# A planner that fixes a fused attention and gated-MLP kernel's order gets new lengths, delays and DMA queue rules

## The chip, the cores and the metric

The kernel runs on one core of one Trainium2 chip. Its time is the device time of one execution in microseconds (us), as a median over several runs. TensorE (PE) multiplies matrices, VectorE (DVE), ScalarE (ACT) and GpSimd (POOL) do element-wise work, SyncE (SP) issues every DMA transfer of this kernel. The five engines run beside each other, each in the order in which its instructions were written, and wait for each other by semaphores.

## The reference

The inputs are q, k, v of 4 batches x 8 heads x 768 positions x 64, and three weight matrices, all float32. What must be computed, cut to what matters:

```python
scores = scale * np.matmul(q, k.transpose(0, 1, 3, 2))
keep = is_sink | in_window          # first n_sink=4 positions, or the last window=128
scores = np.where(keep, scores, -1000000000.0)
a = np.exp(scores - np.max(scores, axis=-1, keepdims=True))
a = a / (np.sum(a, axis=-1, keepdims=True) + 1e-09)
x = np.matmul(a, v).transpose(0, 2, 1, 3).reshape(B * S, H * D)   # 3072 x 512
gate = 1.0 / (1.0 + np.exp(-(x @ w_gate)))                        # 512 x 1536
return gate * (x @ w_val) @ w_out                                 # 1536 x 512
```

## The kernel before

The 3072 tokens are cut into 12 token groups of 256, and those into 8 chunks: four of one group, four of two (`CHUNKS`). For each group there are 8 attention units, one a head, so 96 units `u`. The first 20 units are "plain": float32 matmuls, of which one program row takes two passes in the profile. Later units split each operand into a high and a low half (`hi`, `kl`, `vhl`, `wt`) and run one pass a half. A unit is: load `qkT` and `v` (SP), scores (PE, into PSUM tile `a`), mask and row maximum (DVE, `P`), exp (ACT), reciprocal of the sum (DVE), scaling of `P` (POOL, ACT or DVE), turn (PE transposes `P`), copies and cuts (`wt`: ACT, DVE, POOL), PV (PE, `wt` with `vhl`, and `sk` with `vshl` for the sinks), and two additions (DVE) into `xf`.

The MLP runs over 12 slices `f` of the hidden width. Weights arrive as pairs of 32-bit words (`wst`, 3 buffers, 36 loads of 512 KB) and are decoded by `decode`: load, a multiplication on ACT, a shift (ACT, DVE or POOL), two bit operations on DVE. Chunk 0 (`feed_whole`) uses the decoded weights as they are, `m<-hi,ws` and `o<-ws,th`. `halve` then makes a high half that stays on chip and a low half that goes to DRAM (`wlo_d`); all other chunks load low halves again through 8 buffers `lo` (396 loads of 256 KB). The `lo` buffers lie in memory that the `wst` buffers held, so the first `lo` load (`fetch`, read of `DECODED`) waits for the last decode. `thirds` and the pair chunks are a Strassen-like variant that saves products.

No instruction is placed by hand. `Plan.run` plays the whole program through in a model of its own: each step has a priority, one or more ways (an engine, a length, a function), tiles that it reads and writes, and buffer slots. Whenever a modelled engine is free, the ready step of best priority goes to it, and the sequence in which this happens is the sequence in which the instructions are written. What a step costs is written where it is made (`vec`, `once`, `two`, `act`, `pool`, the numbers in `attend`). `LAT` is the delay from the end of one step to a step that depends on it, `NEXT` the same within one engine, `ISSUE`, `BULK` and the two lines with `dma_free` model the DMA queue. The planner writes filler matmuls (`m<-ident`, 128x128) on PE where PE would be free in its model during the first 130 us and the modelled activity is low. `hint` writes a branch hint on PE, DVE and SP for the branch behind the last instruction (`skip`: it jumps over `general`, which serves inputs of other sizes).

Every step goes through one helper, so nearly all instructions have one line in the profile (L620; L629 after the change), and tiles tell them apart.

Of the kernel before, what the change touches and what calls it, by code (L numbers as in the profile page):

```python
# [59 lines left out]
LAT = 180.0  # L60
BULK = 620.0
ISSUE = 550.0
# [3 lines left out]
NEXT = dict(PE=0.0, V=60.0, A=60.0, G=60.0, Q=0.0)  # L66
# [21 lines left out]
B_lo = 8  # L88
B_w2 = 2
# [223 lines left out]
class Plan:  # L313
# [39 lines left out]
    def run(self, warm, fill_ns, fill):  # L353
# [37 lines left out]
        while events:  # L391
            now = events[0][0]
            while events and events[0][0] <= now:
# [14 lines left out]
                for x in o.after:  # L408
                    x.before -= 1
                    same = len(x.ways) == 1 and x.ways[0][0] == on  # L410
                    x.ready = max(x.ready, now + (NEXT[on] if same else LAT))
                    if on != "PE":
                        x.sure = max(x.sure, now + LAT + (SURE_D if o.dma else SURE))
# [3 lines left out]
            for e in free:  # L417
                if free[e] > now:
                    continue
                held = []  # L420
                unsure = [] if e == "PE" else None
                while waiting[e] or unsure:
# [18 lines left out]
                    if unsure is not None and (  # L441
                        o.sure > now
                        or any(slots[k][v - 1][1] + LAT + SURE > now for k, v in need.items())
                    ):
                        unsure.append((key, o))
                        continue
# [77 lines left out]
                    for x in o.after:  # L524
                        x.todo -= 1
                        x.due = max(x.due, end + LAT)
# [23 lines left out]
def kernel(  # L550
# [84 lines left out]
    def act(cols, psum=False):  # L635
        return 120 + 0.9 * cols

    def pool(cols):
        return Port(170 + 2.17 * cols)
# [199 lines left out]
    WLO, LOADS, GROUPS, DECODED, READY, READY2 = (Fixed(None) for _ in range(6))  # L839

    def sinks(b, u):
        if not b:
# [7 lines left out]
            for t, x in enumerate(VS0):  # L850
                for y in range(2):
                    o = 64 * y + NS * t
                    dma(
                        u + 0.5, 91.0, lambda x=x, y=y, o=o: Q.dma_start(
# [23 lines left out]
    def load(u, b, h, t0, T, prev, L, vraw, vin, qkT, plain):  # L878
# [4 lines left out]
            u, 0.75 * n * R / D, lambda: Q.dma_start(out=qkT()[0:R, 0:n], in_=qk[b, h, 0:R, c0 : c0 + n]),  # L883
# [3 lines left out]
            u, 100.0 * L, lambda: Q.dma_start(  # L887
# [4 lines left out]
    def attend(u, b, h, t0, T, XR):  # L892
# [44 lines left out]
        for t in range(T):  # L937
# [28 lines left out]
            def exp(t=t):  # L966
# [5 lines left out]
            plan.op(u, [("PE", 10 + (4 * n / 2.4 + 6 if plain else 2 * mac(n)), scores)], qk_reads, [sc, (P, t)], busy=0.5 if plain else 0.9)  # L972
            plan.op(
                u, [("V", 260 if first else 535, top)],
                [sc, (MASKS, 3), (MASKS, min(t0 + t, 2))], [sc, (P, t), (NEGM, (u, t))],
            )
            plan.op(u, [("A", 410, exp)], [], [(P, t), (rs, t)])
# [19 lines left out]
        def mul():  # L997
            for t in range(T):
# [4 lines left out]
                ("A", 200, lambda: A.activation(  # L1003
                    out=rs()[:, 0:T], in_=rs()[:, 0:T], func=AF.Copy, scale=1.0, bias=1.0e-9
                )),
                ("G", Port(213), guard(G)), ("V", Port(100), guard(V)),
# [3 lines left out]
            u, [("V", 110, lambda: V.reciprocal(out=rs()[:, 0:T], in_=rs()[:, 0:T]))], [], [rs]  # L1010
        )
        plan.op(u, [("G", Port(660), share), ("A", 720, mul), ("V", Port(555), scale)], [rs], [P])

        if not plain:
# [11 lines left out]
                u, [("V", 180, lambda: V.transpose(  # L1026
# [10 lines left out]
                u, [("G", Port(610), spread(G)), ("V", two(W), spread(V))], [turned, OWN], [sk]  # L1037
# [35 lines left out]
        plan.op(u, [("PE", 30 + (T + plain) * 110, turn)], [P], [tp, wt], busy=0.45)  # L1073
# [11 lines left out]
        plan.op(u, [("G", Port(180 + 0.9 * Z * (T - f) * 128), split)], [], [wt])  # L1085
        plan.op(u, [("G", Port(180 + 0.9 * Z * T * 128), rest_of)], [], [wt])
# [105 lines left out]
        if y:  # L1192
# [8 lines left out]
            elif not pair_of[tn]:  # L1201
# [9 lines left out]
                copy(u, W, hi, xv, read, [(H1, i), (L1, i)], plain)  # L1211
# [44 lines left out]
    def decode(prio, src, whole):  # L1256
# [6 lines left out]
        plan.op(prio, [("Q", ISSUE, lambda: Q.dma_start(out=st(), in_=src))], [], [st], dma=1456.0)  # L1263
# [16 lines left out]
                ("G", Port(1340.0), lambda: G.tensor_scalar(  # L1280
# [38 lines left out]
    def spare(pr, f, k, x):  # L1319
        dma(  # L1320
            pr, 728.0, lambda: Q.dma_start(
# [497 lines left out]
```

## Time and profile before

| what | before |
|---|---|
| median of 3 runs | 771.19 us (770.46 to 771.49) |
| the profiled execution | 774.19 us |
| its span, first to last instruction | 772.5 us |
| PE busy | 749.1 us, 97% of the span |
| DVE, POOL, ACT busy | 607.5, 506.1, 472.0 us |
| mean granted TensorE clock | 0.998 of full speed |

The profile is of one execution, 3.0 us above the median. An engine's busy time includes the tail of each instruction that lies under the next one, so 97% for PE says where PE had something in flight, not that it streamed at its best. Idle time on another engine costs nothing by itself; what counts is whether PE waits.

### The profile page before, as it was taken

The numbers are of one execution on the slowest core, as the hardware profiler recorded it, in microseconds if no ns is written. First come the engines' busy times: TensorE is split into PE (matmuls) and PEld (weight loads), VectorE is DVE, ScalarE is ACT, GpSimd is POOL, SyncE is SP. The second block draws the span as 40 slices with busy tenths as digits, with TensorE's granted clock in tenths as the row PEclk, the third lists the DMA queues.
The fourth block names the chain that finished last, engine by engine and source line by source line (L and its number), as shares of the span: only waits on it lengthen the run. The fifth ranks groups of instructions, "written<-read, shape, count | busy, mean of one in ns | idle before, by whom it ended". The sixth has DMA issues, their size and how long they took to land.

```text
span 772.5 us, 16296 instructions
## 1 busy us (share of the span) xinstructions
PE 749.1 (97%) x4986; PEld 674.9 (87%) x4986; DVE 607.5 (79%) x1782; ACT 472.0 (61%) x1338; POOL 506.1 (66%) x647
## 2 busy tenths in 40 slices
PE   7999999999999999999999999999999999999995
PEld 6866777998989999989999988999999999999995
DVE  5979988996999999969988889778999884433333
ACT  7879888765765777737666665457776652322221
POOL 3654676887999999937777977557976855321210
PEclk9999999999999999999999999999999999999999
DMA  6898987999999877677767777867697655677662
GB/s 165 222 297 250 323 263 234 376 307 311 342 294 319 284 220 207 200 252 231 233 224 225 242 233 222 246 196 251 193 306 249 196 159 178 217 240 211 198 205 86
DMA packets 120879, 185.57 MB, mean 240 GB/s; under 512 B 23248, under 2 KB 45264, under 8 KB 120784
## 3 DMA queue, kind: packets, MB, share of 16 engines
q1 hardware_dynamic: 120784, 184.45, 75.9%
q8 instruction: 42, 0.69, 0.4%
q14 instruction: 53, 0.43, 0.2%
HBM read 159.24 MB, written 25.17 MB: 239 GB/s over the span
## 4 chain that ended last, share of the span: by engine, by line
PE 61%; DVE 11%; DMA 6%; POOL 3%; ACT 2%; issue 2%; SPq 0%; ACTq 0%; POOLq 0%; DVEq 0%
PE m L620 34%; PE a L620 16%; PE o L620 11%; DVE ws L620 2%; DMA wst<-in_moe_w_gate_dram 1%; DMA out_dram<-w 1%; DVE P L620 1%; DVE th L620 1%; DMA vraw<-in_vt_dram 1%; DMA lo<-wlo_d 1%; DVE vhl L620 1%; POOL wt L620 1%; DVE hi L620 1%; DVE gl L620 1%; DVE xf L620 1%
## 5 line engine op out<-in xcount | busy, mean ns | idle before, releaser
L620 PE MATMUL m<-ws,ws 128*128 128x256 f32 x1536 | 290.0, 284 | 0.6 <-DVE th L620 0.2
L620 PE MATMUL m<-ws,lo 128*128 128x256 f32 x1344 | 288.6, 283 | 1.9 <-DMA lo<-wlo_d 1.3
L620 PEld LDWEIGHTS m<-ws,ws 128*128 128x128 f32 x1536 | 244.9, 189 | 13.1 <-DVE th L620 1.0
L620 PEld LDWEIGHTS m<-ws,lo 128*128 128x128 f32 x1344 | 215.0, 189 | 3.1 <-DMA lo<-wlo_d 2.3
L620 POOL TENSOR_SCALAR_AFFINE_SELECT wt<-wt 128x512 fp32r<-128x512 f32 (+3 forms) x192 | 125.9, 657 | 43.5 <-DVE wt L620 18.7
L620 POOL TENSOR_TENSOR gl<-th,gh 128x512 fp32r<-128x512 f32 (+1 forms) x34 | 38.2, 1122 | 99.6 <-ACT gh L620 82.7
L620 ACT ACTIVATE P<-P,negm_all 128x144 f32<-128x144 f32 x192 | 78.9, 412 | 28.7 <-DVE negm_all L620 26.8
L620 ACT ACTIVATE th<-m 128x256 f32<-128x256 f32 x96 | 36.6, 382 | 75.5 <-DVE th L620 71.9
L620 DVE TENSOR_TENSOR cv<-m,cv 128x256 f32<-128x256 f32 x96 | 40.2, 418 | 52.4 <-ACT cv L620 34.8
L620 ACT CAST gh<-th 128x512 fp32r<-128x512 f32 (+1 forms) x82 | 42.9, 523 | 55.3 <-DVE th L620 53.7
L620 POOL TENSOR_TENSOR ws<-ws,ws 128x512 fp32r<-128x512 f32 (+1 forms) x53 | 66.6, 1262 | 9.8 <-DVE ws L620 6.9
L620 PE MATMUL o<-ws,gh 128*128 128x512 f32 x168 | 67.6, 403 | 0.0
L620 PE MATMUL o<-ws,gl 128*128 128x512 f32 x168 | 66.2, 394 | 0.0
L620 PE MATMUL o<-lo,gh 128*128 128x512 f32 x168 | 65.8, 391 | 0.0
L620 DVE CUSTOM_DVE_ANT_0 P<-a,am 128x144 f32<-128x144 f32 x192 | 58.3, 306 | 8.8 <-PE a L620 2.2
L620 PE MATMUL a<-wt,vhl 128*128 128x256 f32 (+2 forms) x282 | 61.0, 327 | 1.8 <-POOL wt L620 1.6
L620 POOL TENSOR_TENSOR kl<-qkT,hi 128x400 fp32r<-128x400 f32 (+1 forms) x56 | 59.2, 1057 | 1.8
L620 PEld LDWEIGHTS a<-wt,vhl 128*128 128x128 f32 x282 | 47.3, 189 | 10.5 <-POOL wt L620 4.1
L620 ACT CAST hi<-qkT 128x656 fp32r<-128x656 f32 (+1 forms) x70 | 49.2, 703 | 10.9 <-PE a L620 10.0
L620 POOL TENSOR_TENSOR P<-P,rs 128x288 f32<-128x288 f32 x46 | 35.1, 764 | 29.8 <-DVE rs L620 26.2
L620 POOL TENSOR_TENSOR hi<-qkT,hi 64x256 fp32r<-64x256 f32 x53 | 41.2, 777 | 14.9 <-issue 4.9
L620 DVE COPY_PREDICATED a<-tri,a 128x128 f32<-128x128 int32 x160 | 45.4, 284 | 3.5 <-PE a L620 3.2
(146 smaller groups left out, 1735.5 us busy)
## 6 DMA issues: line engine op xcount, KB each, us to landing
lo<-wlo_d SPq DMA_DIRECT2D x396, 256.0 KB, 3.7
wlo_d<-ws SPq DMA_DIRECT2D x72, 256.0 KB, 4.3
qkT<-in_qk_dram SPq DMA_DIRECT2D x52, 328.0 KB, 4.1
qkT<-in_qk_dram SPq DMA_DIRECT2D x24, 264.0 KB, 3.5
wst<-in_moe_w_gate_dram SPq DMA_DIRECT2D x12, 512.0 KB, 4.8
wst<-in_moe_w_val_dram SPq DMA_DIRECT2D x12, 512.0 KB, 5.1
wst<-in_moe_w_out_dram SPq DMA_DIRECT2D x12, 512.0 KB, 5.4
out_dram<-w SPq DMA_DIRECT2D x20, 256.0 KB, 4.4
```

Source lines behind the costliest of these rows:

```text
L620: return lambda *a, **kw: tc.keep_in_program_order(op(*a, **kw))
```

## The change

The planner's numbers are replaced. `LAT` (180 ns for all) becomes two tables: `AFTER` by the engine that ends, `TOLD` by the engine that is told. `NEXT`, `ISSUE` and most lengths are new. The DMA model changes: a transfer now ends at the end of the queue plus its length plus `LANDED`, with lengths from `moved` (number of rows a DMA engine, bytes a row), and SP holds a transfer back while the modelled queue is longer than `REACH + QUEUED`. The eight sink loads of a batch (`w<-in_v`) write parts of `VSHL` instead of the whole, so the planner need no longer do them one after the other. `SPLIT` makes copies of later chunks wait for the halves. The branch hint moves from the last slice of the last chunk to the sixth slice from its end. Arithmetic, tiles, buffers and priorities stay.

```diff
-LAT = 180.0
-BULK = 620.0
-ISSUE = 550.0
+AFTER = dict(PE=163.0, V=75.0, A=100.0, G=35.0, Q=0.0)
+TOLD = dict(PE=54.0, V=35.0, A=35.0, G=77.0, Q=27.0)
+REACH = 1800.0
+LANDED = 600.0
+QUEUED = 1000.0
+SHARE = 1.6
+ISSUE = 480.0
-NEXT = dict(PE=0.0, V=60.0, A=60.0, G=60.0, Q=0.0)
+NEXT = dict(PE=0.0, V=10.0, A=25.0, G=0.0, Q=0.0)
...
-                    x.ready = max(x.ready, now + (NEXT[on] if same else LAT))
+                    lat = AFTER[on] + TOLD[x.ways[0][0]]
+                    x.ready = max(x.ready, now + (NEXT[on] if same else lat))
...
+                if e == "Q" and dma_free > now + REACH + QUEUED:
+                    n += 1
+                    heapq.heappush(events, (dma_free - REACH - QUEUED, n, None))
                     continue
...
-                        port = now + ns + (70.0 if e == "V" else 0.0)
+                        port = now + ns + AFTER[e]
...
-                        slow = BULK if o.dma > 1000.0 else 0.0
-                        dma_free = max(dma_free + o.dma, end + 650 + slow + o.dma)
-                        end = dma_free + 750
+                        dma_free = max(dma_free, now + REACH) + o.dma
+                        end = dma_free + LANDED
...
     def act(cols, psum=False):
-        return 120 + 0.9 * cols
+        return 28 + 0.93 * cols
...
+    def moved(n, size):
+        return n * (9 + size / 27.0 + SHARE * size / 160.0)
...
-                u, 91.0, lambda o=o: Q.dma_start(
+                u, moved(8, 256), lambda o=o: Q.dma_start(
                     out=raw()[o : o + NS], in_=v[b, :, 0:NS, :].rearrange("h p d -> p h d"),
-                ), [READY2], [(raw, o)] + [VSHL[b, i] for i in range(2) if b and (b, i) in VSHL],
+                ), [READY2], [(raw, o)] + [(VSHL[b, i], o) for i in range(2) if b and (b, i) in VSHL],
...
-            u, 0.75 * n * R / D, lambda: Q.dma_start(out=qkT()[0:R, 0:n], in_=qk[b, h, 0:R, c0 : c0 + n]),
+            u, moved(R // 16, 4 * n), lambda: Q.dma_start(out=qkT()[0:R, 0:n], in_=qk[b, h, 0:R, c0 : c0 + n]),
...
-        plan.op(u, [("G", Port(660), share), ("A", 720, mul), ("V", Port(555), scale)], [rs], [P])
+        plan.op(u, [("G", Port(621), share), ("A", 625, mul), ("V", Port(555), scale)], [rs], [P])
...
-    plan.op(prio, [("Q", ISSUE, lambda: Q.dma_start(out=st(), in_=src))], [], [st], dma=1456.0)
+    plan.op(prio, [("Q", ISSUE, lambda: Q.dma_start(out=st(), in_=src))], [], [st], dma=moved(8 * n, 8 * m))
...
-            pr, 728.0, lambda: Q.dma_start(
+            pr, moved(8, 2048), lambda: Q.dma_start(
...
+        if ci == len(CHUNKS) - 1 and f == NF - 6:
+            hint([gh], [th], [wol])
...
-        hint([(gh, 1)], [(th, 1)], [wol])
```

What this does to the order is seen at three places. The first is PE where chunk 0 ends and the first product with a low half begins; `a<-hi` and `a<-kl,hi` are scores, `a<-ident,P` a turn, `a<-wt,vhl` and `a<-sk,vshl` PV, `m` and `o` the MLP, `m<-ident` fillers. Before:

```order
L620 MATMUL o_593<-ws_1330,th_1365 128x512
L620 MATMUL m_91<-xf_423,ws_1347 128x256 x2
L620 MATMUL m_92<-hi_270,w_1375 128x256 x2
L620 MATMUL m_92<-xf_423,w_1375 128x256 x2
L620 MATMUL a_1472<-hi_1424 128x272
L620 MATMUL a_1472<-kl_1457,hi_1424 128x272
L620 MATMUL a_1477<-hi_1424 128x272
L620 MATMUL a_1477<-kl_1457,hi_1424 128x272
L620 MATMUL m_91<-ws_620,ws_346 128x256
L620 MATMUL m_91<-ws_623,ws_346 128x256
L620 MATMUL m_91<-ws_620,lo_1435 128x256
```

The same place on PE after the change, from the last turn but one:

```order
L629 MATMUL m_91<-ident 128x128 x9
L629 MATMUL a_1676<-ident,P_1625 128x128 x2
L629 MATMUL m_91<-ident 128x128 x3
L629 MATMUL o_610<-ws_1608,th_1599 128x512
L629 MATMUL o_644<-ws_1608,th_1599 128x512
L629 MATMUL a_1711<-hi_1648 128x144
L629 MATMUL a_1711<-kl_1686,hi_1648 128x144
L629 MATMUL a_1718<-hi_1648 128x272
L629 MATMUL a_1718<-kl_1686,hi_1648 128x272
L629 MATMUL m_91<-ws_638,ws_392 128x256
L629 MATMUL m_91<-ws_649,ws_392 128x256
L629 MATMUL m_91<-ws_638,lo_1698 128x256
```

Ahead of the first `lo` product PE now has three more attention units (turn and PV of each, and scores) and both `o` rows of chunk 0's last slice, and 51 fillers in place of 26: 24 of them stand in the last 40 rows ahead of that product, where there were none.

The second place is SP at the same point: the last `wst` loads, then the first `lo` load. Before:

```order
L620 DMA wst_1305<-in_moe_w_gate_dram 128x4x256
L620 DMA qkT_1319<-in_qk_dram 128x528
L620 DMA wlo_d<-ws_1312 128x512
L620 DMA wst_1340<-in_moe_w_val_dram 128x4x256
L620 DMA wst_1359<-in_moe_w_out_dram 128x1024
L620 DMA wlo_d<-ws_1377 128x512
L620 DMA wlo_d<-ws_1398 128x512
L620 DMA vraw_1426<-in_vt_dram 128x128
L620 DMA lo_1435<-wlo_d 128x512
```

SP at the last `wst` load and behind it, after the change:

```order
L629 DMA wst_1551<-in_moe_w_out_dram 128x1024
L629 DMA wlo_d<-ws_1539 128x512
L629 DMA qkT_1578<-in_qk_dram 128x528
L629 DMA qkT_1602<-in_qk_dram 128x528
L629 DMA vraw_1610<-in_vt_dram 128x128
L629 DMA vraw_1623<-in_vt_dram 128x128
L629 DMA wlo_d<-ws_1613 128x512
L629 DMA w_1642<-in_v_dram 16x8x64 x8
L629 DMA lo_1698<-wlo_d 128x512
```

Ahead of the last `wst` load SP now issues 29 `wlo_d` stores instead of 19, and one `qkT` and one `vraw` load more. Between it and the first `lo` load stand two more `qkT`, one more `vraw` and the eight sink loads of the second batch, which before came one at a time among the later `lo` loads.

The third place is ACT: before the first row of the 36th decode there were 192 rows of the program, and there are 239 now; 18 of the 47 more are casts `ws<-ws` of `halve`, 4 are exps, 6 are scalings of `P`. Over the whole program, 57 rows leave DVE (1905 to 1848), ACT gains 59 and POOL 11; scalings of `P` go from 46 to 33 on POOL, from 22 to 12 on DVE and from 78 to 114 on ACT (two rows a unit there).

## Rows read from the trace of the kernel before

**Rows 1.** The page, part 1: busy time of each engine, share, instructions.

```profile
PE 749.1 (97%) x4986; PEld 674.9 (87%) x4986; DVE 607.5 (79%) x1782; ACT 472.0 (61%) x1338; POOL 506.1 (66%) x647
```

**Rows 2.** Busy time by stage; columns as the first line says.

```profile
core 0: us, PE busy (x) PEld busy (x) DVE busy (x) ACT busy (x) POOL busy (x), PEclk, DMA share, GB/s
0.00:40.00 40.00, 34.58 (x203) 29.78 (x204) 29.63 (x126) 32.87 (x95) 20.55 (x44) 1.00 0.78 198
40.00:126.00 86.00, 81.73 (x374) 60.38 (x373) 74.15 (x196) 74.69 (x144) 49.11 (x58) 1.00 0.88 274
...
140.00:300.00 160.00, 158.11 (x1109) 145.24 (x1108) 143.73 (x409) 107.41 (x336) 143.72 (x181) 1.00 0.90 297
300.00:640.00 340.00, 336.64 (x2372) 313.25 (x2371) 296.01 (x908) 213.32 (x662) 251.52 (x333) 1.00 0.72 225
640.00:764.50 124.50, 124.49 (x852) 114.81 (x850) 50.56 (x111) 31.72 (x73) 29.80 (x22) 1.00 0.63 197
764.50:772.50 8.00, 0.01 (x1) 0.00 (x0) 0.61 (x2) 0.38 (x1) 0.00 (x0) 0.80 0.38 139
```

**Rows 3.** Chain of waits, 110 to 132 us: start, length, what held.

```profile
112.90 5.24 DMA wst<-in_moe_w_gate_dram
...
118.17 0.69 ACT ws L620
...
118.88 1.36 ACT wst L620
...
120.26 0.69 DVE ws L620
...
124.46 1.72 PE o L620 x4
...
128.76 0.57 PE a L620 x4
...
129.98 0.72 PE m L620 x4
```

**Rows 4.** SP in order of time, the last `wst` and first `lo` loads.

```profile
118.95 0.33 SPq L620 DMA_DIRECT2D wst<-in_moe_w_out_dram  x1
...
126.89 3.64 SPq L620 DMA_DIRECT2D lo<-wlo_d  x8
```

**Rows 5.** PE in order of time, one PV and one turn.

```profile
132.96 0.64 PE L620 MATMUL a<-wt,vhl 128*128 128x512 f32 x3
...
133.55 0.40 PE L620 MATMUL m<-ws,ws 128*128 128x256 f32 x2
...
135.70 0.43 PE L620 MATMUL a<-ident,P 128*128 128x128 f32 x2
135.90 0.36 PE L620 MATMUL a<-hi 128*128 128x272 f32 x1
```

**Rows 6.** ACT by form, to 130 us: busy, mean ns, idle ahead.

```profile
L620 ACT CAST ws<-ws 128x512 fp32r<-128x512 f32 x8 | 4.9, 625 | 0.0
```

**Rows 7.** PE's waits, 130 to 640 us: total, times, longest.

```profile
PE m L620 <- DMA lo<-wlo_d: 1.3, 2, 1.0
PE a L620 <- POOL P L620: 0.8, 2, 0.5
```

**Rows 8.** The branch behind the last instruction, and SP's wait there.

```profile
L1771 SPq EVENT_SEMAPHORE  x8: 17/17/17, 770.6 to 771.1; - x8
L1771 DVEq COMPARE_BRANCH  x1: 84/84/84, 765.7 to 765.7; - x1
L1771 DVEq EVENT_SEMAPHORE  x1: 21/21/21, 768.7 to 768.7; - x1
SPq L1771 <- SPq L1771: 2.9, 1, 2.9
```

**Rows 9.** The last stores: when issued; their size and median time to landing.

```profile
764.11 3.48 SPq L620 DMA_DIRECT2D out_dram<-xf  x4
out_dram<-xf SPq DMA_DIRECT2D x4, 256.0 KB, 3.3
```

More of the change, by code (lines that the diff above doesn't have):

```diff
@@ L88 @@
 B_lo = 8
+GUARD = 0
 B_w2 = 2
@@ L442, in run @@
                         o.sure > now
-                        or any(slots[k][v - 1][1] + LAT + SURE > now for k, v in need.items())
+                        or any(slots[k][v - 1][1] + AFTER["V"] + TOLD["PE"] + SURE > now for k, v in need.items())
                     ):
@@ L525, in run @@
                         x.todo -= 1
-                        x.due = max(x.due, end + LAT)
+                        x.due = max(x.due, end + AFTER[e] + TOLD[x.ways[0][0]])
                         if not x.todo and x.ways[0][0] in soon:
@@ L838 @@
     X0 = {}
-    WLO, LOADS, GROUPS, DECODED, READY, READY2 = (Fixed(None) for _ in range(6))
+    WLO, SPLIT, GROUPS, DECODED, READY, READY2 = (Fixed(None) for _ in range(6))
     def sinks(b, u):
@@ L853, in sinks @@
                     dma(
-                        u + 0.5, 91.0, lambda x=x, y=y, o=o: Q.dma_start(
+                        u + 0.5, moved(4, 256), lambda x=x, y=y, o=o: Q.dma_start(
                             out=x()[o : o + NS, :, y * D : y * D + D],
@@ L886, in load @@
         dma(
-            u, 100.0 * L, lambda: Q.dma_start(
+            u, moved(8 * L, 256) if plain else moved(8, 256 * L), lambda: Q.dma_start(
                 out=vin(), in_=vt[b, h, :, k0 // 128 : k0 // 128 + L]
@@ L970, in exp @@
                 )
-            plan.op(u, [("PE", 10 + (4 * n / 2.4 + 6 if plain else 2 * mac(n)), scores)], qk_reads, [sc, (P, t)], busy=0.5 if plain else 0.9)
+            plan.op(u, [("PE", (10 + 4 * n / 2.4 + 6 if plain else 249 if n > 256 else 177), scores)], qk_reads, [sc, (P, t)], busy=0.5 if plain else 0.9)
             plan.op(
-                u, [("V", 260 if first else 535, top)],
+                u, [("V", 222 if first else 545, top)],
                 [sc, (MASKS, 3), (MASKS, min(t0 + t, 2))], [sc, (P, t), (NEGM, (u, t))],
             )
-            plan.op(u, [("A", 410, exp)], [], [(P, t), (rs, t)])
+            plan.op(u, [("A", 405, exp)], [], [(P, t), (rs, t)])
         def guard(E):
@@ L1036, in attend @@
             plan.op(
-                u, [("G", Port(610), spread(G)), ("V", two(W), spread(V))], [turned, OWN], [sk]
+                u, [("G", Port(568), spread(G)), ("V", two(W), spread(V))], [turned, OWN], [sk]
             )
@@ L1071, in rest_of @@
             )
-        plan.op(u, [("PE", 30 + (T + plain) * 110, turn)], [P], [tp, wt], busy=0.45)
+        plan.op(u, [("PE", 20 + T * 60 + 190 * plain, turn)], [P], [tp, wt], busy=0.45)
         plan.op(
@@ L1328, in halve @@
         hi, lo = slot(F32R, shape), slot(F32R, shape)
-        copy(pr, 512, hi, whole, [whole, *r], [hi, (lo, 0)], start=start)
+        copy(
+            pr, 512, hi, whole, [whole, *r], [hi, (lo, 0)] + [(SPLIT, (f, k))] * (k > 2), start=start
+        )
         rest(pr, 512, lo, whole, hi, [whole, hi], [(lo, 0)])
@@ L1390, in out_tiles @@
                 plan.op(-1000.0 + ci + 1, ways if last else ways[:1], [acc], [ot])
-            dma(ci, 728.0, lambda ot=ot, r=r: Q.dma_start(out=out[r : r + 128], in_=ot()), [ot])
+            dma(ci, moved(8, 2048), lambda ot=ot, r=r: Q.dma_start(out=out[r : r + 128], in_=ot()), [ot])
     def feed(ci):
@@ L1466, in fetch @@
             LAST[0] = dma(
-                pr, 728.0, lambda x=x, k=k: Q.dma_start(
+                pr, moved(8, 2048), lambda x=x, k=k: Q.dma_start(
                     out=x().bitcast(F32), in_=wlo_d[f, :, k * 512 : k * 512 + 512]
```

21 lines of the change are left out of this document (11 added, 10 removed).

## The prediction

> **What bounds the kernel now.** I read four views, in this order: the page's busy times, the busy times by stage, the chain of waits around the place that the order moves most, and the waits of PE alone. PE has work in flight for 749.1 of 772.5 us [rows 1]; no other engine is over 79%. By stage [rows 2] PE's idle time is 5.4 us before 40 us, 4.3 us from 40 to 126, 1.9 us from 140 to 300, 3.4 us from 300 to 640, nothing from 640 to the last product at 764.5, and then there is a tail of 8.0 us without PE. So the kernel is PE's work plus some 15 us of waits and a tail. [...] The change adds no product but fillers; it can win back waits and the tail, or add waits. It cannot win much over 20 us, whatever it does to the other engines.
>
> Two stages differ from the rest. From 40 to 126 us DVE and ACT are busy 74 to 75 of 86 us and DMA 88%: here the weights are decoded, and PE gets a slice's products when a decode ends. The chain there [rows 3] goes round one loop: a weight load takes 5.24 us to land, then ACT 0.69, ACT 1.36 and DVE 0.69 us, and then its buffer takes the next load. That is 8.0 us a turn with three buffers, 2.7 us a decode, for 36 decodes. The first load of a low half goes out at 126.89 [rows 4], and the first product with it is in the PE row that starts at 129.98 [rows 3]. From there on PE always has MLP work of a started chunk beside attention.
>
> **Part 1: up to the first product with a low half.** The new order gives PE more to do ahead of it: three units and the two `o` rows of a slice. Four score products took 0.57 us [rows 3], a turn 0.20 (135.70 to 135.90) and a PV with its sink row 0.59 (132.96 to 133.55) [rows 5], so 1.36 us a unit and 4.1 us for three; the last two `o` rows, four passes, took 1.72 us [rows 3]. That is 5.8 us of PE work which is only moved: it is missing later. So the first such product may come at 129.98 + 5.8 = 135.8 us without loss, and what it comes later or earlier is lost or won, since PE has work behind it and nothing to start before it. The 25 more fillers are not counted: they stand where the planner saw PE free, and matter only if it is not.
>
> When does it come? By three counts, with ends far apart. By the loop: when the queue is kept short a load lands sooner. At 1 us less of 5.24 a turn is 7.0 us; 36 decodes, three beside each other, are 12 turns, so up to 12 us. But PE, busy 82 of 86 us there, could not keep up, so I take 130 us as the low end (5.8 us won). By DMA: ahead of the last weight load SP issues ten 256 KB stores and a `qkT` and a `vraw` load more, about 2.96 MB; at 274 GB/s [rows 2] that is 10.8 us, so 140.8 us if the queue is the bound all the time. By ACT: 47 instructions more stand ahead of the last decode, 18 of them casts of 625 ns [rows 6], 11 us, and the rest about 8 us at 0.2 to 0.4 us each (an estimate from the steps in rows 3): 19 us, so 149 us if ACT's idle time stays what it was. But ACT idled 11.3 of 86 us from 40 to 126 [rows 2], and the casts were put there because ACT was free while a load was under way. I take 137 us, between the loop's end and the DMA's, nearer to neither: a loss of 1.2 us, with ends of -5.8 and +13.2. What is queued behind a decode that ACT reaches late is the buffer's next load, and then chunk 1 as a whole.
>
> The 0 to 40 us stage keeps its order on PE up to small swaps, with 27 fillers there in place of 26; I count 0.
>
> **Part 2: 130 to 640 us.** Here the delays matter: the planner puts a step of PE where its inputs should be ready, and the trace shows where they were not. PE idles 5.3 us from 140 to 640 [rows 2]. The largest items are loads of `lo`, 1.3 us at two places, and turns that waited for the scaling of `P` on POOL, 0.8 us [rows 7]. Of both kinds the change takes some away: 13 of the 46 scalings leave POOL and go to ACT, which is busy 213 of 340 us in the long stage against POOL's 252 and DVE's 296 [rows 2], and a load behind a shorter queue is late less often. But what stands in the old order was late for reasons a model with right lengths would not fully remove, as a DMA's time varies. And delays of 70 ns (POOL to DVE) to 240 ns (PE to POOL) in place of 180 let the planner set a turn and its PV a little closer than before; each new miss costs 0.3 to 1.0 us, as the old ones did. Bounds: at best all 5.3 us go; at worst some ten new misses add 4 us. I take 2.9 us won, over half of what is there. If ACT's cover is gone in a stage where it serves exps as well, the scalings are late there instead, and this is the +4 end.
>
> **Part 3: the other steps.** Edits of lengths have no cost of their own beyond parts 1 and 2. The 57 rows that leave DVE are worth nothing directly: DVE waits for PE, and PE has other work. The eight sink loads in one run (32 KB each) go out ahead of the first `lo` load, 8 issues at some 0.45 us a piece (3.64 us for eight `lo` issues [rows 4]); SP waits there for the last decode anyway, so 0, and up to 3.6 us inside part 1's range if it does not.
>
> **Part 4: the tail.** SP issues the last four stores from 764.11 to 767.59, and a store lands 3.3 us after its issue [rows 9]: the last near 770.2. SP's wait instructions behind the branch begin at 770.6, and it lost 2.9 us between its own branch and them [rows 8]. If the earlier hint lets SP pass the branch at once, the end is bounded by the landing: 0.4 us, and with the waits that could then run ahead of it 0.6 us. DVE had a hint too and still stood 3.0 us between its branch at 765.7 and its next instruction at 768.7 [rows 8], so a hint alone does not do it. I take 0.3 us, ends 0 and 0.6.
>
> [...]
>
> **Sum.** +1.2 - 2.9 + 0 - 0.3 = -2.0 us. The profiled execution took 774.19 us for a span of 772.5 and so becomes 772.2; it stands 3.0 us above the median of 771.19, which becomes 769.2 us.
>
> **Rivals.**
> - *The gap before the first low half decides; slower.* The planner itself put 24 fillers into the last 40 rows before that product, and it does so only where it sees PE free: with true DMA lengths it expects the decodes to come late. For it: 10.8 us of DMA and 19 us of ACT work moved ahead. Against it: those are moved into idle time of ACT and a DMA that was 88% busy. At 145 us the loss is 9.2 us, and 9.2 - 2.9 - 0.3 = +6.0: 777.2 us. It decides from 140.5 us on, where the loss outweighs the other terms by 1.5 us.
> - *Nothing to be measured.* The first product comes near 137 us and as many new misses come as old ones go: +1.2 - 1.2 - 0.2 = -0.2: 771.0 us. For it: PE is 97% busy, and the waits are many and small. Here the change would not do what it says.
> - *The short queue pays in full.* Loads land a microsecond sooner, the first product comes at 131 us, and most waits of part 2 go: -4.8 - 4.5 - 0.3 = -9.6: 761.6 us. For it: 5 us of landing for loads in a stage with 88% DMA. Against it: there the bytes are the bound, and they stay.
>
> **How the numbers follow.** Forecast 0.35, slower rival 0.30, no change 0.20, full gain 0.15. A measurement of this kernel can tell some 0.2%, 1.5 us, from no change. Faster by more than that: 0.35 less 0.04 for a forecast case that falls short, plus 0.15: 0.46. Within: 0.20 and that 0.04, less 0.04 from the edges: 0.20. Slower: 0.34. The forecast's own range is 766 to 771 us. The ends of all terms together give 759.5 to 788.4; 8 in 10 are held by 761 to 778, which leaves out the far half of the ACT count and the full sum of all best ends.
>
> **What would show it right or wrong.** Part 1: the start of the first `m<-ws,lo` row on PE: 137 us by the forecast, 145 by the slower rival, 131 by the full gain; with it the landing of `wst` loads from 40 to 126 us, now 5.0 us in the chain, under 4.5 if the queue is shorter. Part 2: PE's idle time from 140 to 640 us at 2.4 us instead of 5.3, with no `lo` among the longest waits. Part 4: the time between SP's branch and its first wait behind it, 2.9 us now. The forecast is wrong if the first low product comes after 140 us, or if PE's idle time from 140 to 640 grows; then the time is above 771. It is wrong too if PE's own work takes longer, which would be seen from 640 us on, where there is now no idle time at all.

## The result, and the profile after

The changed kernel takes 781.52 us (median of 4 runs, 780.24 to 782.53) against 771.34 us for the kernel before, run beside it: 1.0117 times, 95% interval 1.0069 to 1.0165. It is slower, and the forecast of 769.2 us with its range of 761 to 778 us does not hold it. The profiled executions differ by 6.05 us (774.19 and 780.24; spans 772.5 and 778.5); the medians differ by 10.2 us, because the profiled execution of before lay 2.9 us above its median and that of after 1.3 us below. The traces explain the 6 us; the other 4.1 us between the medians stand in no trace. One execution of e4 and one of e9, below, took 4182 us, for a reason that is not known, and are left out of all figures.

Busy time by stage after the change, in the columns of [rows 2]; the last stage ends with the span.

```profile
0.00:40.00 40.00, 34.15 (x200) 28.79 (x201) 28.58 (x121) 32.46 (x98) 18.47 (x39) 1.00 0.79 206
40.00:126.00 86.00, 83.38 (x402) 64.16 (x400) 73.19 (x199) 83.34 (x173) 69.42 (x79) 1.00 0.92 284
...
140.00:300.00 160.00, 157.66 (x1121) 146.95 (x1121) 130.26 (x364) 100.36 (x306) 131.28 (x167) 1.00 0.90 294
300.00:640.00 340.00, 335.52 (x2349) 309.88 (x2349) 288.75 (x899) 227.41 (x714) 263.45 (x345) 1.00 0.71 223
640.00:764.50 124.50, 124.50 (x865) 115.83 (x865) 48.54 (x106) 30.88 (x71) 23.20 (x18) 1.00 0.68 209
764.50:778.50 14.00, 7.01 (x40) 5.77 (x38) 4.38 (x10) 2.49 (x6) 0.00 (x0) 0.93 0.21 78
```

Read against [rows 2]: from 40 to 126 us ACT's idle time fell from 11.3 to 2.7 us, filled with work that the planner put ahead of the decodes, and POOL went from 49 to 69 us. PE's idle time from 140 to 640 us grew, from 5.3 to 6.8 us (2.34 + 4.48), but 0.7 us of that is the gap in front of the first product with a low half, shown next. From that product to 300 us PE idles 1.6 us, and 1.9 before (rows of before and after):

```profile
129.98:300.00 170.02, 168.12 (x1172) 153.70 (x1173) 152.60 (x433) 115.06 (x357) 152.67 (x189) 1.00 0.91 299
```

```profile
143.24:300.00 156.76, 155.16 (x1111) 145.61 (x1112) 127.14 (x353) 98.88 (x302) 128.47 (x163) 1.00 0.91 295
```

With the stage to 640 us that makes 6.1 us (1.60 + 4.48) for 5.3.

PE in order of time around the first product with a low half (start, length; in brackets the idle time before it and what ended it):

```profile
142.10 0.40 PE L629 MATMUL m<-ws,ws 128*128 128x256 f32 x2
143.24 0.39 PE L629 MATMUL m<-ws,lo 128*128 128x256 f32 x1 [0.74 <-DMA lo<-wlo_d]
```

It starts at 143.24 us, 13.3 us later than in [rows 3]. SP ahead of it, which answers to [rows 4]:

```profile
127.58 0.33 SPq L629 DMA_DIRECT2D wst<-in_moe_w_out_dram  x1
...
129.05 3.11 SPq L629 DMA_DIRECT2D qkT<-in_qk_dram  x2
133.85 0.80 SPq L629 DMA_DIRECT2D vraw<-in_vt_dram  x2
...
136.14 3.75 SPq L629 DMA_DIRECT2D w<-in_v_dram  x8
140.00 5.05 SPq L629 DMA_DIRECT2D lo<-wlo_d  x9
```

The last weight load goes out 8.6 us later than before, and between it and the first `lo` load lie 12.4 us, where there were 7.9. Two things end this wait almost together. One is the run of eight sink loads, to 139.89. The other is the last step of the last decode, the second `ws` row here, which ends at 139.75; DVE in order of time:

```profile
136.68 0.42 DVE L629 TENSOR_TENSOR low<-a,low 64x256 f32<-64x256 f32 x1 [0.97 <-ACT low L629]
...
138.20 0.41 DVE L629 TENSOR_SCALAR ws<-ws 128x512 int32<-128x512 int32 x1
138.65 1.10 DVE L629 SCALAR_TENSOR_TENSOR ws<-wst,ws 128x512 int32<-128x512 int32 x1
```

ACT had done its part of this decode by 134.5. DVE reached the rest 3.7 us later, since the new order has attention steps ahead of it. One of them waited 0.97 us for ACT's `low`, and the decode, written behind it on DVE, was held back with it.

ACT itself came late. Its steps of the last decode and DVE's last one, before:

```profile
123.85 0.68 ACT L620 ACTIVATE ws<-wst 128x512 f32<-128x512 f32 x1
...
124.56 1.36 ACT L620 ACTIVATE wst<-wst 128x512 uint16<-128x512 uint16 x1
...
126.18 0.68 DVE L620 SCALAR_TENSOR_TENSOR ws<-wst,ws 128x512 int32<-128x512 int32 x1
```

ACT's two steps after the change:

```profile
132.46 0.67 ACT L629 ACTIVATE ws<-wst 128x512 f32<-128x512 f32 x1
133.16 1.36 ACT L629 ACTIVATE wst<-wst 128x512 uint16<-128x512 uint16 x1
```

ACT starts on it 8.6 us later, and DVE, which ended 0.9 us behind ACT, now ends 5.2 us behind it, 4.3 us more. These two make 12.9 of the 13.3 us by which the product is late. Busy time from 40 us to ACT's start on the last decode, before and after (ACT is the fourth column of busy time):

```profile
40.00:123.85 83.85, 79.58 (x368) 59.33 (x366) 72.00 (x193) 72.56 (x141) 47.03 (x56) 1.00 0.90 279
```

```profile
40.00:132.46 92.46, 89.29 (x429) 68.24 (x427) 79.19 (x213) 89.68 (x189) 75.07 (x84) 1.00 0.92 286
```

ACT does 17.1 us more work ahead of that decode. Its idle time took in 8.5 us of it (11.3 to 2.8), and the other 8.6 us are the delay. What ACT waited for from 40 to 126 us, weight loads alone, before and after:

```profile
ACT ws L620 <- DMA wst<-in_moe_w_val_dram: 5.2, 5, 2.2
ACT ws L620 <- DMA wst<-in_moe_w_gate_dram: 1.9, 3, 0.9
ACT ws L620 <- DMA wst<-in_moe_w_out_dram: 1.7, 3, 0.7
```

```profile
ACT ws L629 <- DMA wst<-in_moe_w_out_dram: 0.2, 1, 0.2
```

So before, ACT stood 8.8 us of this stage for the weight loads of the loop in [rows 3]; now it hardly stands for them, and the loop goes at the pace of ACT's own work. The loads did not land sooner either: the `wst` rows of this stage have medians of 5.3, 4.7 and 5.6 us from issue to landing, against 5.0, 4.9 and 5.0 us before.

To compare orders I split the time of each kernel at that product. From its start I take off the PE work that stands ahead of it, each product at its median distance to the next one in the trace of before and fillers at nothing; what is left is the loss in front, start-up included. The same from there to the last product gives the loss behind. Both are read from one execution, and these differ: the profiled one of before lay 2.9 us above its median, that of e6 below 4.9 us. Before has 130.0 - 106.5 = 23.5 us in front and 14.5 behind, after 143.2 - 112.0 = 31.2 and 13.8. So the change lost 7.8 us in front and won 0.8 behind, which is less than two executions differ by, and 1.0 us in the tail (last product to the end, 8.4 to 7.4 us): +6.0 us, the difference of the spans.

SP at the last stores and at the branch behind the last instruction, which answers to [rows 8] and [rows 9]:

```profile
771.12 2.89 SPq L629 DMA_DIRECT2D out_dram<-xf  x4
...
L1786 SPq EVENT_SEMAPHORE  x8: 17/17/17, 774.6 to 777.2; - x8
...
L1786 SPq COMPARE_BRANCH  x1: 70/70/70, 774.1 to 774.1; - x1
```

0.5 us lie between branch and first wait, where there were 2.9. Of the 1.0 us won in the tail, 0.6 come from the four stores, which SP issued in 2.89 us where it took 3.48, and 0.4 from what stands behind them.

### The profile page after: what moved, and what is told of

It reads as the page before. It is cut to its first block, busy times and chain, and to the rows that moved or that the text cites. A ratio compares the mean times of both kernels' runs of the same rounds, so it can differ in the third digit from the quotient of the medians.

```text
span 778.5 us, 16396 instructions
## 1 busy us (share of the span) xinstructions
PE 754.9 (97%) x5036; PEld 681.2 (88%) x5036; DVE 585.6 (75%) x1725; ACT 489.5 (63%) x1397; POOL 518.4 (67%) x658
## 4 chain that ended last, share of the span: by engine, by line
PE 70%; DVE 5%; POOL 3%; ACT 2%; DMA 1%; issue 1%; SPq 0%; DVEq 0%; POOLq 0%; ACTq 0%
PE m L629 39%; PE a L629 18%; PE o L629 13%; DVE th L629 1%; DMA lo<-wlo_d 1%; DVE ws L629 1%; POOL wt L629 1%; DVE P L629 1%; DMA out_dram<-w 1%; POOL ws L629 1%; SPq L629 0%; ACT P L629 0%; DVE low L629 0%; DVE vhl L629 0%; DVE wt L629 0%
## 5 line engine op out<-in xcount | busy, mean ns | idle before, releaser
L629 POOL TENSOR_TENSOR gl<-th,gh 128x512 fp32r<-128x512 f32 (+1 forms) x49 | 55.2, 1127 | 127.9 <-ACT gh L629 117.1
L629 POOL TENSOR_TENSOR ws<-ws,ws 128x512 fp32r<-128x512 f32 (+1 forms) x61 | 75.0, 1240 | 4.7 <-DVE ws L629 3.4
L629 POOL TENSOR_TENSOR kl<-qkT,hi 128x400 fp32r<-128x400 f32 (+1 forms) x57 | 57.6, 1011 | 2.0
L629 POOL TENSOR_TENSOR hi<-qkT,hi 64x256 fp32r<-64x256 f32 x58 | 47.1, 812 | 14.6 <-DVE xf L629 2.9
L629 ACT ACTIVATE wst<-wst 128x512 uint16<-128x512 uint16 x34 | 46.3, 1361 | 0.5
```

The lines of the kernel that those rows point to most:

```text
L629: return lambda *a, **kw: tc.keep_in_program_order(op(*a, **kw))
```

## The experiments

All were timed against the kernel before on the same chip. T is the theory that the new picture of the DMA queue makes the planner expect the decodes late and put other work ahead of them; R1 lays the loss on the new delays and lengths of the engines, R2 on the run of sink loads, R3 on any change of numbers at all. The results first; "lo" is the start of the first product with a low half, and the last three columns are in us, from each kernel's profiled execution.

| kernel | us | ratio to before (95%) | lo | in front | behind |
|---|---|---|---|---|---|
| before (its profile) | | 1 | 130.0 | 23.5 | 14.5 |
| after (its profile) | 781.5 | 1.0117 (1.0069 to 1.0165) | 143.2 | 31.2 | 13.8 |
| e1 before, DMA picture new | 797.2 | 1.0296 (1.0256 to 1.0336) | 143.7 | 32.1 | 27.3 |
| e2 after, DMA picture old | 783.5 | 1.0111 (1.0059 to 1.0163) | 139.2 | 28.8 | 20.0 |
| e3 after, sinks one by one | 802.8 | 1.0360 (1.0318 to 1.0403) | 142.6 | 30.5 | 36.7 |
| e4 before, hint early | 773.9 | 1.0003 (0.9978 to 1.0027) | 129.0 | 22.4 | 14.2 |
| e5 after, decodes urgent | 787.5 | 1.0205 (1.0166 to 1.0244) | 135.8 | 26.2 | 25.1 |
| e6 before, delay 182 | 781.3 | 1.0118 (1.0084 to 1.0153) | 135.0 | 26.2 | 24.1 |
| e7 before, delay 178 | 780.4 | 1.0102 (1.0064 to 1.0139) | 137.8 | 29.6 | 14.8 |
| e8 after, delays old | 810.3 | 1.0496 (1.0453 to 1.0538) | 154.6 | 42.6 | 31.7 |
| e9 before, margin 606 | 772.8 | 0.9984 (0.9956 to 1.0012) | 131.0 | 24.5 | 12.0 |
| e10 before, issue 545 | 779.6 | 1.0064 (1.0033 to 1.0095) | 135.6 | 26.1 | 18.6 |
| e11 after, PE delay 161 | 798.7 | 1.0293 (1.0248 to 1.0338) | 143.0 | 31.8 | 32.5 |
| e12 after, start 1782 | 790.2 | 1.0203 (1.0158 to 1.0247) | 140.5 | 29.8 | 22.9 |
| e13 after, transfers 80% | 793.5 | 1.0280 (1.0241 to 1.0320) | 139.8 | 32.2 | 24.4 |
| e14 after, transfers 70% | 799.9 | 1.0347 (1.0308 to 1.0387) | 141.9 | 34.5 | 32.0 |
| e15 as e2, PE delay 161 | 783.8 | 1.0159 (1.0117 to 1.0202) | 136.4 | 26.0 | 21.3 |
| e16 as e1, delay 178 | 796.9 | 1.0324 (1.0284 to 1.0363) | 142.8 | 31.2 | 27.7 |
| e17 after, no cap | 797.8 | 1.0304 (1.0260 to 1.0348) | 150.6 | 38.2 | 21.7 |
| e18 as e1, no cap | 809.8 | 1.0449 (1.0402 to 1.0495) | 140.7 | 29.3 | 44.4 |

**Halves of the change.** The kernel before with the new DMA picture alone (`moved`, `ISSUE`, the two lines with `dma_free`, the hold on SP), and the kernel after with the old one. Of the edit, the two lines:

```diff
-                        slow = BULK if o.dma > 1000.0 else 0.0
-                        dma_free = max(dma_free + o.dma, end + 650 + slow + o.dma)
-                        end = dma_free + 750
+                        dma_free = max(dma_free, now + REACH) + o.dma
+                        end = dma_free + LANDED
```

> The kernel before, its planner given only the change's picture of the DMA queue (lengths of transfers from rows and bytes, start after 1800, landing 600, SP held when the queue is 1000 ahead, issue 480); delays and lengths of engines as before. Theory T (the DMA picture makes the planner expect the decodes late, so that it puts other work ahead of them, and the first product with a low half comes late): that product at 140 to 144 us instead of 129.98, time 777 to 782 us, ratio 1.008 to 1.014. Rival R1 (the new delays and lengths of the engines do it): the product at 130 to 134 us, time 769 to 773. Rival R3 (any change of the planner's numbers shuffles the order and loses something): anywhere from 772 to 780, with no tie to that product.

> The kernel after, its planner given back the old picture of the DMA queue; the new delays and lengths of engines, the earlier hint and the rest of the change stay. Theory T: the first product with a low half at 130 to 135 us, and with the tail 1 us shorter a time of 768 to 772 us, ratio 0.996 to 1.002. Rival R1: the product still at 140 to 144 us, time 777 to 782. Rival R3: 772 to 780 with no tie to that product.

The DMA picture alone puts the product at 143.7 us, as T has it, but costs 3%, more than the whole change. All but the DMA picture still loses 1.1%, with the product at 139.2 and more lost behind, near to what R1 has. Each half loses by itself, so T or R1 alone does not do, and R3 could no longer be left aside.

**The sink loads.** After, with the sinks chained in the plan as before:

```diff
-                ), [READY2], [(raw, o)] + [(VSHL[b, i], o) for i in range(2) if b and (b, i) in VSHL],
+                ), [READY2], [(raw, o)] + [VSHL[b, i] for i in range(2) if b and (b, i) in VSHL],
```

> The kernel after, with the eight sink loads of 32 KB ordered among each other in the plan as before, so that they no longer stand in one run ahead of the first load of a low half (two of them do). Theory T: the last decode ends at 139.75 us anyway and bounds that load, so the time is that of after, 780 to 782 us, first product with a low half 142 to 144. Rival R2 (the run of eight issues, 3.75 us of SP, holds the low half): the product 2 to 3.5 us earlier, 140 to 141 us, and the time 777 to 779.

R2 falls: the product comes 0.7 us earlier, not 2 to 3.5. But its ratio is 2.4 points above after's, which no theory expected. SP in order of time, PE's waits from 140 to 180 us, and the busy time by stage there:

```profile
135.90 0.42 SPq L629 DMA_DIRECT2D w<-in_v_dram  x1
...
139.57 6.18 SPq L629 DMA_DIRECT2D lo<-wlo_d  x10
...
160.71 0.91 SPq L629 DMA_DIRECT2D w<-in_v_dram  x2
```

```profile
PE a L629 <- POOL vshl L629: 12.0, 1, 12.0
```

```profile
152.00:156.00 4.00, 0.96 (x8) 0.64 (x6) 3.77 (x13) 1.63 (x7) 1.69 (x3) 0.85 0.91 302
156.00:160.00 4.00, 0.00 (x0) 0.00 (x0) 1.34 (x4) 1.26 (x2) 3.09 (x5) 0.50 0.59 165
...
164.00:168.00 4.00, 2.66 (x7) 1.97 (x8) 2.00 (x5) 1.18 (x3) 3.03 (x5) 0.50 0.21 73
168.00:172.00 4.00, 4.00 (x15) 3.34 (x15) 2.94 (x11) 3.15 (x9) 2.91 (x6) 0.52 0.24 81
172.00:176.00 4.00, 4.00 (x30) 3.70 (x29) 3.78 (x13) 3.23 (x13) 3.47 (x6) 1.00 0.48 134
```

The last sink loads go out at 160.7, behind the `lo` loads; PE stands 12 us in front of the PV that reads them. While it stands its granted clock falls to 0.50, and in the stretch from 168 to 172, at 0.52, it starts 15 products in 4.00 busy us where it starts 30 from 172 on, at 1.00. In this order the run of eight sink loads is no cost but what keeps PE fed. e16 and e18, where the sinks are chained too, show the same wait (14.7 and 12.3 us); e1, also chained, does not.

**The hint.** The kernel before with the hint moved. The few steps that work out the branch's flag follow it, as in the change: the first of them starts at 723 us here and at 664 us before, which the expectation overlooks.

```diff
+        if ci == len(CHUNKS) - 1 and f == NF - 6:
+            hint([gh], [th], [wol])
...
-        hint([(gh, 1)], [(th, 1)], [wol])
```

> The kernel before, with only the branch hints moved to the slice at which the change puts them (near 728 us instead of 753 to 761); every other instruction stays. If the hint's place shortens the tail: SP from its branch to its first wait 0.5 us instead of 2.9, the end 1.0 us earlier, 770.2 us, ratio 0.998 to 0.9995. If the instruction layout of the changed order does it, and the hint's place nothing (ACT has no hint and got quick too): 2.9 us stays, time 771.2, ratio 0.9995 to 1.0005.

The branch and SP's first wait behind it:

```profile
L1772 SPq EVENT_SEMAPHORE  x8: 17/17/17, 768.8 to 769.4; - x8
...
L1772 SPq COMPARE_BRANCH  x1: 70/70/70, 765.6 to 765.6; - x1
```

3.2 us, near the 2.9 of before: the hint's place does nothing for SP here, and the time is the same. SP passed its branch in 0.5 us in after and e5 alone; in the ten other kernels with the early hint it took 2.9 to 3.4 us. The expectation's other reading, the instruction layout, was not tried by itself. On DVE the matter is open: it took 0.6 us in nine of the twelve kernels with the early hint and in none of the eight with the late one, but 3.3 us in e4.

**Decodes more urgent.**

```diff
-DS1 = 8.0
+DS1 = 4.0
```

> The kernel after, with one number changed: the decodes of the weights are four units more urgent in the plan (DS1 4 for 8), so that fewer steps stand ahead of them. Theory T (what stands ahead of the decodes makes the first product with a low half late, and that is what the time lost): that product at 130 to 136 us instead of 143.2, time lower than that of after by 4 to 8 us, ratio to before 1.000 to 1.006. Rival R3 (any change of the planner's numbers shuffles the order and loses something): a ratio of 1.005 to 1.025, whatever that product does.

The front does what T says: the product comes at 135.8 us and 5.0 of the 7.8 us lost in front are back. ACT's work from 40 us to its start on the last decode, and SP's first `lo` load:

```profile
40.00:123.23 83.23, 81.26 (x388) 62.66 (x387) 73.80 (x195) 80.21 (x177) 57.37 (x65) 1.00 0.93 282
```

```profile
128.88 3.64 SPq L629 DMA_DIRECT2D lo<-wlo_d  x8
```

With 9.5 us less of ACT's work ahead of it than in after, ACT starts on that decode 9.2 us earlier, and the load goes out at 128.9 us for 140.0. The time does not follow, since 11.3 us more are lost behind. Busy time by stage of e5 at the place where most of it goes:

```profile
328.00:332.00 4.00, 1.77 (x10) 1.31 (x9) 3.82 (x17) 3.10 (x12) 3.70 (x7) 1.00 0.82 272
332.00:336.00 4.00, 0.95 (x3) 0.49 (x3) 3.59 (x5) 3.51 (x10) 3.57 (x4) 0.79 0.56 143
336.00:340.00 4.00, 2.69 (x13) 2.62 (x13) 3.27 (x4) 1.85 (x4) 4.00 (x4) 0.50 0.07 18
```

PE idles 5.3 of 8 us, with DVE, ACT and POOL busy; its longest waits there are 2.7 us for the halves `ws` that ACT makes of the next chunk's `xf` and 2.6 us for `P` from POOL. Then its clock falls to 0.50. Here one chunk's products have run out before the next chunk's input is ready. e1, e8, e11 and e12 lose time, with the clock at 0.50, at the same place.

**One number moved by 1%, old planner.**

```diff
-LAT = 180.0
+LAT = 182.0
```

e7 has `LAT = 178.0` there instead, and e10 only this:

```diff
-ISSUE = 550.0
+ISSUE = 545.0
```

> The kernel before with one number of the planner changed by 1%: the delay between engines 182 in place of 180, which has nothing to do with what the change meant. Theory T: the first product with a low half stays at 129 to 133 us and the time within 0.4% of before. Rival R3: a loss of 0.5 to 2%, from waits that appear somewhere behind 140 us; then a part of what the change lost is the price of any new order, as the old one was the better of many.

> As the one with 182, to the other side: 178 in place of 180. Theory T: within 0.4% of before. Rival R3: a loss of 0.5 to 2%, at other places than with 182.

> The kernel before with the time that SP takes to issue a weight load at 545 in place of 550 in its planner: another order from the first rows on. Theory T: first product with a low half at 130 to 135 us (2.9 us more work stands ahead of it), ratio 0.997 to 1.004. Rival R3: ratio 1.005 to 1.02.

None of these edits has to do with what the change meant, and each costs 0.6 to 1.2%: R3 holds. e7 is the cleanest case: with nothing else of the change, the product comes 7.8 us later, 6.1 us more are lost in front and 0.3 behind, and the ratio is 1.0102. PE around that product in e7:

```profile
135.75 1.98 PE L620 MATMUL o<-ws,th 128*128 128x512 f32 x4 [0.21 <-DVE th L620]
...
137.81 0.28 PE L620 MATMUL m<-ws,lo 128*128 128x256 f32 x1
```

A fourth number left PE's order as it was until far behind that product:

```diff
-SURE = 600.0
+SURE = 606.0
```

> The kernel before with one margin of its planner at 606 in place of 600. On PE the order is the same for the first 1044 of 4916 rows (the first product with a low half is row 244), and another one behind. Theory T (the loss is made in front of the first product with a low half, and nearly only there): that product at 129 to 131 us and a ratio of 0.998 to 1.003. Rival R3 (the old order was the best of many, and any other loses all along): the product at 129 to 131 us and still a ratio of 1.004 to 1.012, from new waits behind 200 us.

The product stays at 131.0 us and the time is that of before. Of the rivals T is the nearer here: with the old front, another order behind need not lose. One such order does not show that none would; e6 lost 9.6 us behind, in an execution that lay 4.9 us above its median.

**One number moved by 1%, new planner.**

```diff
-AFTER = dict(PE=163.0, V=75.0, A=100.0, G=35.0, Q=0.0)
+AFTER = dict(PE=161.0, V=75.0, A=100.0, G=35.0, Q=0.0)
```

e12 has this alone:

```diff
-REACH = 1800.0
+REACH = 1782.0
```

> The kernel after with one of its new delays changed by 1% (behind PE 161 in place of 163): another order of the changed planner. If the changed planner's orders lose by its DMA picture (theory T): first product with a low half again at 140 to 146 us, and a ratio to before of 1.008 to 1.02. If what after lost is the price of any new order and no more (R3): a ratio anywhere from 1.002 to 1.025, about that of the old planner's other orders (1.010 and 1.012 for its delay at 178 and 182).

> As the one with 161: the kernel after with one number of its DMA queue changed by 1% (a transfer starts after 1782 in place of 1800). Theory T: first product with a low half at 140 to 146 us, ratio 1.008 to 1.02. R3: 1.002 to 1.025, with no tie to that product.

Both are slower than after itself, by 1.8 and 0.9 points of the ratio. The product comes where T has it, but e11's ratio lies above both expectations and e12's within R3's alone. The changed kernel is itself a good draw among the orders of its planner.

**The old delays in the new planner.**

```diff
-AFTER = dict(PE=163.0, V=75.0, A=100.0, G=35.0, Q=0.0)
-TOLD = dict(PE=54.0, V=35.0, A=35.0, G=77.0, Q=27.0)
+AFTER = dict(PE=180.0, V=180.0, A=180.0, G=180.0, Q=180.0)
+TOLD = dict(PE=0.0, V=0.0, A=0.0, G=0.0, Q=0.0)
```

> The kernel after, its planner given back the one delay of 180 between all engines (and none for the DMA queue beyond it); the new picture of the DMA queue, the new lengths and the rest stay. Theory T (the DMA picture): the first product with a low half still at 141 to 146 us, time 779 to 786. If the new delays are what costs: that product at 130 to 135 us and the time within 0.4% of before.

Neither: 1.0496, with the product at 154.6 us. In this one order the old delays with the new DMA picture are worse than the new ones, so nothing here says that the new delays are what costs. But the edit does more than its expectation says. The changed planner also adds `AFTER` to the time for which its model holds `port`, which marked steps of DVE and POOL (`Port`) take in turn there: 180 for both here, where the old planner had 70 and 0. So this is not the old delays alone, and how much is due to which is open.

**Shorter transfers in the plan.** Theory D: the longer transfers alone make the orders poorer. In e14 the factor is 0.7.

```diff
-        return n * (9 + size / 27.0 + SHARE * size / 160.0)
+        return 0.8 * n * (9 + size / 27.0 + SHARE * size / 160.0)
```

> The kernel after, its planner told that every transfer is 20% shorter than the change's formula says; start, landing, cap, delays and engine lengths stay as changed. Theory D (the longer transfers in the plan are what hurts: the planner then expects the decodes late and puts other work ahead of them): the first product with a low half at 129 to 133 us, loss in front of it 24 to 26 us, ratio 0.998 to 1.006. Rival (the changed planner's orders are poorer for another reason, its delays, cap or start): the product at 138 to 145 us or, if earlier, a ratio still of 1.015 to 1.03 from what comes behind it.

> As the one with 80%, with transfers 30% shorter: another order of the same kind. Theory D: product at 129 to 133 us, ratio 0.998 to 1.008. Rival: as there, 1.015 to 1.03.

Theory D falls, though half of it holds. The plan does put less ahead (107.6 and 107.3 us of PE work), and the decodes are nearly back in time: the first `lo` load goes out at 130.97 us in e13 and at 127.13 in e14, where before had 126.89.

```profile
130.97 3.17 SPq L629 DMA_DIRECT2D lo<-wlo_d  x7
```

```profile
127.13 3.65 SPq L629 DMA_DIRECT2D lo<-wlo_d  x8
```

The product still comes at 139.8 and 141.9 us: now PE itself is late with what stands ahead of it, busy 78.10 of 86 us from 40 to 126 in e13 where after had 83.38. From 40 to 142 us its longest waits in e13 are for `wt` and `P` from POOL, 3.4 and 3.0 us.

```profile
40.00:126.00 86.00, 78.10 (x362) 57.33 (x361) 70.13 (x182) 76.51 (x155) 51.20 (x65) 1.00 0.89 270
```

**Second orders of the two halves.** e15 is e2 with `PE=161.0` in `AFTER`, e16 is e1 with `LAT = 178.0`.

> The kernel after with the old picture of the DMA queue, and one new delay at 161 in place of 163: a second order of that planner (the first gave 1.011 and the product at 139.2 us). Theory D: no clock fall behind 300 us and a ratio of 1.002 to 1.013, as the old planner's other orders. Rival: 1.015 to 1.03.

> The kernel before with only the new picture of the DMA queue, and its delay at 178 in place of 180: a second order of that planner (the first gave 1.030 and the product at 143.7 us). Theory D: product at 140 to 146 us, ratio 1.012 to 1.035. Rival (the 1.030 was a bad draw of a planner no worse than the old): ratio 1.002 to 1.013.

1.0159 for e15 lies just inside the rival's range, its interval in part below, and no clock falls behind 300 us, as D had it; 1.0324 for e16 is as D had it, so e1's 1.0296 was not a bad draw by itself. D itself falls with e13 and e14, but the two pictures still differ. By now there are five whole new orders for each DMA picture: 1.0064, 1.0102, 1.0111, 1.0118, 1.0159 with the old one (e10, e7, e2, e6, e15; mean 1.011) and 1.0117, 1.0203, 1.0293, 1.0296, 1.0324 with the new one (after, e12, e11, e1, e16; mean 1.025). Only after itself reaches into the old ones' range. What the traces show is where the others lose: in e1, e11 and e12 at the place near 336 us, with the clock at 0.50 for 7 to 17 us, and in e16 behind the late sinks, for 17 us. Of the five with the old picture only e6 has such falls behind the first low product, two of 3.4 us.

**The cap.**

```diff
-QUEUED = 1000.0
+QUEUED = 1.0e9
```

> The kernel after without the cap in its planner that holds SP when the DMA queue is 1000 ahead; the new lengths, start and landing of transfers stay. So far five orders with the new DMA picture gave 1.012 to 1.032 of before, five with the old one 1.006 to 1.016. If the cap makes the orders poorer: 1.004 to 1.016, without a wait of over 2 us behind 140 us. If the new lengths of transfers with their start and landing do: 1.018 to 1.035.

> The kernel before with only the new DMA picture, without its cap: the second draw for the same question, on the old delays. Cap: 1.004 to 1.016. Lengths, start and landing: 1.018 to 1.035, as with the cap (1.030 and 1.032).

Without the cap 1.0304 and 1.0449, the second above both ranges: taking the cap away mends nothing. What stays is the lengths of transfers with their start and landing, and `ISSUE`. Which of these makes the orders poorer is not settled: shorter lengths alone (e13, e14) did not mend it, and start, landing and `ISSUE` were not tried by themselves in the new picture, but for the 1% of e12.

## Why the prediction was wrong

**Part 1 failed, by its size.** Its frame held: what the product comes later, less the work that was only moved, is lost (13.3 - 5.8 = 7.5 us by the prediction's count, 7.8 by the split above, where it had 1.2). The failed step is "I take 137 us, between the loop's end and the DMA's, nearer to neither". It lets ACT's idle time take in all the work that was moved ahead, as "the casts were put there because ACT was free while a load was under way". ACT got 17.1 us more, near the 19 counted; its idle time took in 8.5 us, half of it, and ACT came to the last decode 8.6 us late. e5 bears this out from the other side: 9.5 us less, and 9.2 us earlier. What no count had was the last link, DVE's end behind ACT's, 4.3 us longer than before. I counted work ahead on ACT and DMA, and not the waits that stand ahead on each engine in turn.

The low end rested on loads that land a microsecond sooner behind a shorter queue. That a load lands later behind others is in the trace of before: the first three weight loads, issued one behind another from 8.71 to 9.95 us, took 4.3, 5.1 and 6.9 us to land. After the change they landed no sooner, and a sooner landing would have won little, as ACT waited 0.2 us for them. The DMA count of 140.8 us was the nearest of the three, but by luck: with the queue as the bound, ACT would have waited for loads.

**Part 2 won nothing.** The failed step is "I take 2.9 us won". PE's idle time from 140 to 640 us went up by 1.6 us, and from the first low product on by 0.8 us. By the split, the loss from that product to the last fell by 0.8 us. So the term is about nothing, and its sign is not settled. PE's waits there, which answer to [rows 7]:

```profile
PE a L629 <- DVE wt L629: 1.8, 2, 1.4
PE o L629 <- DVE gl L629: 1.2, 1, 1.2
PE m L629 <- DMA lo<-wlo_d: 0.7, 1, 0.7
```

The one wait for `lo` is the gap in front of the first low product. Those of before behind it are gone, and those for `P` from POOL left the longest, as foreseen; new ones for DVE took their place.

Of the 8.0 us between the forecast's -2.0 and the +6.0 of the spans, part 1 has 6.6 and part 2 has 2.1; the tail gives 0.7 back. The medians differ by another 4.1 us, of which no trace shows the place.

**Part 3** held for after as it stands: the sinks, SP's last work ahead of the product, cost at most the 0.7 us of e3. That chaining them would cost 2.4 points was not seen.

**Part 4** had the sign, -1.0 us against -0.3, but not the cause: e4 moved the hint and SP's 2.9 us stayed (3.2), and 0.6 of the 1.0 us lie in the issue of the stores.

**The rivals.** "The gap before the first low half decides" named the place (145 us; 143.2 measured) and the loss: +6.0 us, just what the spans differ by, though the median is 781.5 us and not its 777.2. That the sum hits is in part luck, as its terms were 9.2, -2.9 and -0.3 us for 7.8, -0.8 and -1.0. Nor was it the DMA that held the decodes, as it had it: ACT waited 0.2 us for loads. It had 0.30 against 0.35 for the forecast; its sign, 24 fillers that the planner itself put ahead of that product, was the best evidence that I had, and I set it back behind idle time on other engines. A rival was missing altogether: that almost any new order loses, because the present one is better than its neighbours, as if picked from many. Three changes of a number by about 1% cost 0.6 to 1.2%, and a fourth, which left the front as it was, gained nothing that can be told. A loss of that size is nearly all of after's 1.2%. That the new DMA picture is worse still, 2.5% on average over five orders, does not show in after, which is a good draw.

No version measured here beats the kernel before; e4 and e9 equal it.

## What to carry to other kernels

Where a greedy planner sets the order, a change of any of its numbers draws a new order. Move a number by 1% in both planners and compare the families, not one draw of each with the best of many; and count on a loss for the first new draw. New lengths and delays, meant to be truer, did not give better orders here. To predict such a change, follow the one chain that decides (here the last decode) through each engine's written order, with the waits ahead of it, and do not let all of an engine's idle time stand for slack: of 17.1 us that ACT got here, half fitted in.

## What the runs showed of the hardware

PE's 12 us wait in e3 cost more than itself: the granted clock fell to 0.50 and stayed there until about 172 us, 7 us into PE's work again, and 15 products took the 4 us that later held 30. SP's time across the same branch had two values over twenty kernels, 0.5 us twice and 2.9 to 3.4 us eighteen times, and the place of the hint did not decide which.
